# A recurrent attention and a silu layer on one core: the first eight units in another order on all engines, u loaded as one row

## The chip, the cores and the metric

The kernel runs on one core of a Trainium2 chip. The metric is the device time of one execution in microseconds (us), as the median of several runs. Engines are named as in the profile: PE (TensorE; PEld is its weight load), DVE (VectorE), ACT (ScalarE), POOL (GpSimd) and SP (SyncE, which here only issues DMAs).

## The reference

A linear attention with a decayed state is followed by a two-layer network. All inputs and the output are float32; batch 4, 8 heads, 768 steps, head size 48, hidden size 2048.

```python
def _attn_ref(r, k, v, w, u):
    state = zeros((B, H, D, D)); y = zeros_like(r)
    for t in range(S):
        kt, vt, rt = k[:, :, t], v[:, :, t], r[:, :, t]
        cur = einsum('bhd,bhe->bhde', u[None] * kt, vt)
        y[:, :, t] = einsum('bhd,bhde->bhe', rt, state + cur)
        state = w[None, :, :, None] * state + einsum('bhd,bhe->bhde', kt, vt)
    return y

def _moe_ref(x, w_in, w_out):          # x: y as (3072, 384)
    h = x @ w_in
    return (h * (1.0 / (1.0 + exp(-h)))) @ w_out
```

## The kernel before, in words

The sequence is cut into 6 chunks of 128 steps. A unit is one chunk of one batch entry with all 8 heads; unit i is chunk i // 4 of batch entry i % 4, so there are 24 units, and the first eight are the first two chunks. Each unit loads three tiles of 192 KB (`rin`, `kin`, `vin`, in 8 buffers each).

For a unit, PE turns r and k (line 258, 16 transposes: T), DVE multiplies them by powers of w (line 270: rT, kT), PE multiplies r by k (line 321 for the first four units, P or A; line 394 for the others in pairs, D), DVE masks the product (n, m), and PE multiplies it by v (V, or Z with the state). The term with u goes another way: POOL multiplies k by r (line 226, ku) and by u (line 231, ru), DVE sums over the head (line 239, rd), POOL multiplies v by that sum (line 244, vu), and DVE adds it when it takes y from PSUM (line 342: e, z). POOL also decays k for the state (line 234, kc); PE sums k times v into states (S for the first chunk, Q later). ACT casts v (v16), evicts the transposed y (xT) and applies silu. y is turned on PE (line 525, yT) for the first six units, and by DMA later.

The network's first layer on a chunk (line 540: L and H) needs y of that chunk turned and a quarter of w_in (i_q0 to i_q3; the steps with the numbers 12 to 15 use the last quarter); its silu is G. The second layer (line 562) needs w_out (i_o0 to i_o3). POOL issues the weights, each as a DMA that casts to float16. SP issues the loads of r, k and v.

The instructions of each engine run in the order in which the program states them; there is no scheduler. For the first eight units that order is one written list of words (`order`, near line 650): a word names a step and a unit, and each step's instructions go to the end of their engines' queues. Behind the list a loop takes the units from the seventh on in pairs, and fills TensorE's time with pieces of the two layers left over (`fillers`). `n*spin` puts n matmuls on idle data on PE; `clear` is four such matmuls. A load is `lr`, `lk` or `lv` on SP's queue; `ak` is k on ACT's queue. At most eight of these DMAs are in flight: each takes one of eight semaphores in turn, and its queue waits until the DMA that had it before has landed. PSUM tiles tagged "moe" share four buffers in the order of the list.

`pd`, `pa` and `kz` clear the pads of the 48-wide heads (rin and kin on DVE or ACT, kc on POOL); `cz` clears tiles for pairs of states; `mh` makes maskH from maskM on POOL by two copies. The powers of w come from `wpT` (two small loads), over `lnw` (ACT: logarithm and lamR), `eK` (DVE) and `lamK` (ACT); `wr` loads w as one row, which `wb` spreads over 128 partitions by a matmul with ones.

Of the kernel before, what the change touches and what calls it, by code (L numbers as in the profile page):

```python
# [15 lines left out]
def kernel(  # L16
# [175 lines left out]

    def spread_u():
        nc.scalar.dma_start(out=u_bc, in_=bass.AP(tensor=u.tensor, offset=0,
                                                  ap=[[0, 128], [D, H], [1, D]]))

    def copy_u(copy=nc.vector.tensor_copy):
# [35 lines left out]
    def decayed_k(i, eng=nc.gpsimd):  # L233
        eng.tensor_tensor(out=kc[i % NIN][:, :, 0:D], in0=kin[i % NIN][:, :, 0:D],  # L234
                          in1=lamH if unit(i)[0] else lamC, op=ALU.mult)

# [14 lines left out]
    def turn_one(i, x):  # L251
# [3 lines left out]
        for p in range(NP):  # L255
            for y in range(2):
                rows = slice(HC * y, HC * y + HC)
                nc.tensor.transpose(L(i)["t"][0:PR, y, x, p, :], flat[rows, 128 * p:128 * p + PR],  # L258
                                    ident[rows, rows])

    def decay_one(i, x, key=None):
# [6 lines left out]
        lam = (lam[:, :, 0:HC].unsqueeze(1).broadcast_to([PR, 2, NP, HC]) if unit(i)[0]  # L268
               else lam.rearrange("p g (y t) -> p y g t", y=2))
        nc.vector.tensor_tensor(  # L270
            out=L(i)[key].rearrange("p g (y t) -> p y g t", y=2),
            in0=L(i)["t"][0:PR, :, x], in1=lam, op=ALU.mult)

    def early(i):
        return unit(i)[0] == 1

# [25 lines left out]

    def cast_r(i, copy=nc.vector.tensor_copy):
        L(i)["rT16"] = wrk.tile([PR, NP, C], F16, name="rT16", bufs=4)
        copy(out=L(i)["rT16"], in_=L(i)["rT"])

# [69 lines left out]
    def spread_first(i, copy=nc.vector.tensor_copy):  # L376
        spread_pairs(copy, carry_pairs[i // 2], L(i)["sps"])

# [46 lines left out]
    def w_half():  # L425
        return wHT.unsqueeze(1).unsqueeze(3).broadcast_to([PR, 2, NP, D])

    def state_first(i):
        s1 = L(i)["s1"] = wrk.tile([PR, 2, NP, D], FP, name="s1")
        nc.vector.tensor_tensor(out=flat(s1), in0=L(i)["sp"][0][0:PR, 0:HD],  # L430
                                in1=flat(L(i)["sdec"]), op=ALU.add)
        if early(i):
            spread_pairs(nc.scalar.copy, inner_pairs[i // 2 % 2], s1)
            return
        for j in range(2):
            spread_state(nc.scalar.copy, j, inner[i // 2 % 2], s1)

    def state_second(i):
        sc, b = unit(i)
        if sc == NCH - 1:  # L440
            return
        s2 = L(i)["sp"][1][0:PR, 0:HD].rearrange("p (e g n) -> p e g n", e=2, g=NP)
        for p in range(NP):
            nc.vector.scalar_tensor_tensor(
                out=st[b // 2][:, :, p, :], in0=L(i)["s1"][:, :, p, :], scalar=wHT[:, p:p + 1],
                in1=s2[:, :, p, :], op0=ALU.mult, op1=ALU.add)

# [17 lines left out]
    def outputs_halves(i):  # L465
# [8 lines left out]
        if early(i):  # L474
            for p in range(NP):
                for e in range(2):
                    for x in (e, 1 - e):
                        s = inner_pairs[i // 2 % 2] if x else carry_pairs[i // 2 - 2]
# [11 lines left out]
        for p in range(NP):  # L490
            for j in range(2):
                h = 2 * p + j
                for e in range(2):
                    for x in range(2):
                        r = HC * x
                        nc.tensor.matmul(place(e, x, D * h, D), L(i)["am2"][r:r + HC, j, e, p, :],  # L496
                                         L(i + e)["v16"][r:r + HC, h, :],
                                         start=False, stop=True, skip_group_check=True)

# [122 lines left out]
    def piece(word, f):  # L622
# [5 lines left out]
        "id16": lambda: nc.gpsimd.tensor_copy(out=ident16, in_=ident), "itr": row_numbers,  # L628
        "itc": column_numbers, "mk": mask, "mh": half_mask, "wr": lambda: row(w_row, w),
        "lnw": powers_r, "eK": exponents_k, "lamK": powers_k,  # L630
        "wb": lambda: spread_row("w", w_row), "lnwb": ln_w, "lamC": powers_c, "lamH": powers_h,
        "tab": silu_table, "ud": spread_u, "clear": clear, "spin": lambda: None,
        "H": lambda: halved.pop(0)(),
    }
    unit_steps = {
        "T": turn, "rT": lambda i: decay_one(i, 0), "kT": lambda i: decay_one(i, 1),
        "v16": cast_v, "kc": decayed_k, "vu": bonus_v, "ku": bonus_ku, "ru": bonus_rku,
        "rd": bonus_sum, "D": product_halves, "A": lambda i: product(i, i + 1), "n": masked,
        "m": masked_halves, "V": outputs_y, "e": evict_first, "S": first_sums, "st": first_state,
        "sc": spread_first, "yT": turn_y, "xT": copy_x,  # L640
        "xTD": lambda i: copy_x(i, nc.vector.tensor_copy),
        "rA": lambda i: cast_r(i, nc.scalar.copy), "sd": decayed_state, "i_q": ld_win,
        "i_o": ld_wout, "Q": sums, "s1_": state_first, "s2_": state_second, "sn": next_state,
        "sx": next_crossed, "Z": outputs_halves, "z": evict_halves, "lr": lambda i: ld(i, rin, r),
        "lk": lambda i: ld(i, kin, k), "lv": lambda i: ld(i, vin, v),
        "ak": lambda i: ld(i, kin, k, nc.scalar), "pd": pad, "pa": pad_copy,
        "kz": lambda i: nc.gpsimd.memset(kc[i][:, :, D:64], 0.0), "cz": zero_state,
    }
    order = """
        id itr itc lr0 mk id16 wr ak0 ud lr1 lk1 lv0 kz2 lr2 lv1 pd1 pd2 lv2 lk2 cz2 pd0 lr3  # L650
        lk3 kz3 cz1 kz0 kz1 pd3 cz3 kz5 kz6 kz7 cz0 mh lnw eK kz4 lv3 lamK clear lr4 lk4 lv5
        lv4 lr5 lk5 lr6 lk6 lk7 lr7 6*spin lv7 lv6 T0 ku0 rT0 kT0 3*spin T1 rT1 kT1 v160 ru0
        rd0 ku1 pa5 wb v161 A0 ru1 rd1 n0 vu0 lnwb lamC vu1 lamH tab pa4 pa6 pa7 n1 2*spin
        V0 e0 i_q0 T2 kT2 4*spin V1 ku2 yT0 ru2 rT2 xTD0 T3 rT3 e1 i_q1 1*spin yT1 xT1 v162
        kT3 ku3 ru3 rd2 A2 vu2 i_q2 3*spin v163 rd3 vu3 n2 n3 L0.0 G0.0 V2 L0.2 G0.2 e2 V3
        e3 L0.4 yT2 G0.4 kc1 xT2 yT3 kc0 xT3 L0.6 G0.6 S0 sc0 st0 kc2 L2.2 L2.0 L2.4 T4 L2.6
        rT4 kT4 kc3 G2.0 G2.2 ku4 G2.4 v164 G2.6 L4.8 S2 sc2 st2 i_q3 ru4 rA4 G4.8 L4.10
        L4.9 rd4 kc5 sd4 G4.10 L4.11 T5 G4.9 kc4 G4.11 vu4 ku5 kT5 ru5 i_o0 rT5 v165 Q4 D4
        s1_4 m4 rd5 s2_4 rA5 L4.12 G4.12 vu5 i_o1 L4.13 G4.13 Z4 z4 L4.14 G4.14 L4.15 G4.15
        yT4 xT4 i_o2 yT5 xT5 T6 kT6 v166 rT6 kc6 ku6 rA6 H H ku7 H kc7 T7 rT7 v167 rA7 H kT7  # L660
        H ru7 ru6 rd6 sd6 i_o3 vu6 sn4 sx4
    """
    for word in order.split():
# [85 lines left out]
```

## Time and profile before

| | |
|---|---|
| median of 3 runs | 189.76 us (189.26 to 190.07) |
| the profiled execution's own time | 190.19 us |
| its span in the trace | 188.5 us |
| TensorE busy | 178.8 us (95%) |
| VectorE, ScalarE, GpSimd busy | 115.8, 108.0, 111.3 us |
| read from HBM, written | 20.65 MB, 4.72 MB |

Times in a timeline or a chain count from the start of the span. In a timeline row stand the start, the length, the engine (an engine's name with q is its instruction queue, where DMAs are issued), the line, the operation, what it writes and reads, how many, and in brackets how long the engine stood before it and what it waited for. In a group row stand the total, the mean of one in ns, and the idle time before them.

### The profile page before, as it was taken

The page shows a single profiled execution, that of the slowest core. Times are in us where ns is not written, and L with a number is a line of the kernel's source. Part 1 is how long each engine was busy: PE and PEld are TensorE (multiplying, and loading weights), DVE is VectorE, ACT ScalarE, POOL GpSimd, SP SyncE. Part 2 cuts the span into 40 slices and gives each one's busy share as a digit, 9 for nine tenths or more (in the row PEclk, how much of TensorE's full clock was granted, in tenths as well). Part 3 has the DMA queues.
Part 4 walks back from the last instruction along what each step waited for, and adds up shares of the span by engine and source line. Part 5 has one row for each costly group of instructions (what it writes and reads, how often), then busy time and mean ns, then how long its engine had stood idle before and what let it go on. Part 6 is the DMA issues. An engine that isn't in the chain of part 4 may idle for free.

```text
span 188.5 us, 6820 instructions
## 1 busy us (share of the span) xinstructions
PE 178.8 (95%) x2915; PEld 117.3 (62%) x2915; DVE 115.8 (61%) x221; ACT 108.0 (57%) x214; POOL 111.3 (59%) x145
## 2 busy tenths in 40 slices
PE   7788999999899999999999999999999999999992
PEld 2355885679666896656656655656746666555662
DVE  7389847857796693697675696755883955000120
ACT  5157569569433397158695268695268592289200
POOL 8599997799899837738639547659349130000000
PEclk9999999999999999999999999999999999999998
DMA  5899999999959368369177287185386201410012
GB/s 88 170 200 181 230 182 185 180 211 193 187 101 207 139 129 164 109 132 208 46 145 172 68 164 193 37 175 129 89 168 171 45 3 45 125 42 0 17 70 85
DMA packets 88737, 24.44 MB, mean 130 GB/s; under 512 B 83329, under 2 KB 88194, under 8 KB 88706
## 3 DMA queue, kind: packets, MB, share of 16 engines
q1 hardware_dynamic: 84992, 20.39, 49.5%
q0 software_dynamic: 2176, 3.15, 10.3%
q10 hardware_dynamic: 1538, 0.46, 1.1%
q8 instruction: 23, 0.38, 0.8%
q14 instruction: 8, 0.07, 0.1%
HBM read 20.65 MB, written 4.72 MB: 135 GB/s over the span
## 4 chain that ended last, share of the span: by engine, by line
PE 84%; DMA 8%; DVE 3%; ACT 2%; issue 1%; SPq 1%; DVEq 0%
PE ops L562 32%; PE hps L540 32%; DMA kin<-in_k_dram 8%; PE att L258 6%; PE att L394 4%; PE att L321 2%; PE yp L487 2%; PE sp L417 2%; PE ops L587 1%; PE yp L496 1%; PE zs L167 1%; DVE kT L270 1%; DVE am L327 1%; PE yp L337 1%; ACT gT L549 1%
## 5 line engine op out<-in xcount | busy, mean ns | idle before, releaser
L540 PE MATMUL hps<-xT,win 128*128 128x512 f16 (+1 forms) x360 | 66.6, 337 | 0.1
L549 ACT ACTIVATE gT<-hps 128x512 f16<-128x512 f32 x96 | 56.0, 597 | 14.7 <-PE hps L540 11.3
L562 PE MATMUL ops<-wout,gT 128*128 128x384 f16 x368 | 62.5, 326 | 0.0
L540 PEld LDWEIGHTS <-win 128*128 128x128 f16 x360 | 38.9, 114 | 21.3 <-issue 0.3
L562 PEld LDWEIGHTS <-gT 128*128 128x128 f16 x368 | 35.2, 98 | 23.3
L244 POOL TENSOR_TENSOR vu<-vin,rku 128x384 f32<-128x384 f32 x24 | 19.6, 830 | 28.0 <-DVE rku L239 27.5
L270 DVE TENSOR_TENSOR rT<-att,lamR 112x512 f32<-112x512 f32 (+1 forms) x40 | 27.1, 685 | 6.7 <-PE att L258 6.2
L226 POOL TENSOR_TENSOR ku<-kin,rin 128x384 f32<-128x384 f32 x24 | 24.1, 1006 | 9.6 <-DMA kin<-in_k_dram 9.5
L568 ACT COPY osb<-ops 128x384 f32<-128x384 f32 x20 | 9.6, 479 | 34.5 <-issue 18.1
L342 DVE TENSOR_TENSOR y<-yp,vu 64x384 f16<-64x384 f32 (+1 forms) x34 | 18.9, 555 | 14.9 <-PE yp L496 6.8
L231 POOL TENSOR_TENSOR rku_f<-ku,u_bc 128x384 f32<-128x384 f32 x24 | 24.0, 1001 | 2.1 <-DMA u_bc<-in_u_dram 0.5
L234 POOL TENSOR_TENSOR kc<-kin,lamH 128x384 f16<-128x384 f32 x20 | 20.1, 1005 | 0.7 <-DMA kin<-in_k_dram 0.6
L270 DVE TENSOR_TENSOR kT<-att,lamK 112x512 f32<-112x512 f32 x24 | 16.3, 681 | 1.5 <-PE att L258 1.5
L249 ACT CAST v<-vin 128x384 f16<-128x384 f32 x24 | 11.5, 512 | 6.6 <-DMA vin<-in_v_dram 6.4
L430 DVE TENSOR_TENSOR s<-sp,sdec 112x384 f32<-112x384 f32 x10 | 5.6, 557 | 15.9 <-PE sp L417 15.7
L570 DVE COPY osb<-ops 128x384 f32<-128x384 f32 x3 | 1.7, 558 | 21.3 <-PE ops L562 21.3
L401 DVE TENSOR_TENSOR am<-att,maskH 128x1024 f16<-128x1024 f32 x10 | 12.2, 1218 | 1.5 <-PE att L394 1.5
L239 DVE TENSOR_REDUCE rku<-rku_f 128x8 f32<-128x384 f32 x24 | 12.4, 544 | 0.6 <-POOL rku_f L231 0.6
L394 PE MATMUL att<-rT,kT 48*64 48x64 f32 x640 | 11.8, 220 | 0.3 <-DVE rT L270 0.3
L258 PE MATMUL att<-ident,rin 64*112 64x64 f32 x192 | 10.3, 228 | 1.0 <-DMA rin<-in_r_dram 1.0
L373 ACT CAST s1h<-s 48x384 f16<-48x384 f32 x16 | 8.2, 510 | 5.4 <-DVE s L430 5.2
L394 PEld LDWEIGHTS att<-rT,kT 48*64 48x64 f32 x640 | 10.5, 135 | 0.5 <-DVE rT L270 0.5
(83 smaller groups left out, 173.8 us busy)
## 6 DMA issues: line engine op xcount, KB each, us to landing
rin<-in_r_dram SPq DMA_DIRECT2D x24, 192.0 KB, 4.3
vin<-in_v_dram SPq DMA_DIRECT2D x24, 192.0 KB, 4.1
kin<-in_k_dram SPq DMA_DIRECT2D x23, 192.0 KB, 4.3
out_dram<-osb SPq DMA_DIRECT2D x23, 192.0 KB, 3.0
win<-in_moe_w_in_dram POOLq DMA_DIRECT2D x4, 384.0 KB, 6.2
wout<-in_moe_w_out_dram POOLq DMA_DIRECT2D x4, 384.0 KB, 6.3
xT<-y SPq DMA_TRANSPOSE x18, 2.4
kin<-in_k_dram ACTq DMA_DIRECT2D x1, 192.0 KB, 4.1
```

What stands on the lines that cost most here:

```text
L226: eng.tensor_tensor(out=L(i)["ku"], in0=kin[i % NIN][:, :, 0:D], in1=rin[i % NIN][:, :, 0:D], op=ALU.mult)
L231: eng.tensor_tensor(out=L(i)["rku_f"], in0=L(i)["ku"], in1=u_bc, op=ALU.mult)
L234: eng.tensor_tensor(out=kc[i % NIN][:, :, 0:D], in0=kin[i % NIN][:, :, 0:D], in1=lamH if unit(i)[0] else lamC, op=ALU.mult)
L239: nc.vector.tensor_reduce(out=L(i)["rku"], in_=L(i)["rku_f"], axis=mybir.AxisListType.X, op=ALU.add)
L244: eng.tensor_tensor(out=L(i)["vu"], in0=vin[i % NIN], in1=L(i)["rku"].unsqueeze(2).broadcast_to([128, H, D]), op=ALU.mult)
L258: nc.tensor.transpose(L(i)["t"][0:PR, y, x, p, :], flat[rows, 128 * p:128 * p + PR], ident[rows, rows])
L270: nc.vector.tensor_tensor(out=L(i)[key].rearrange("p g (y t) -> p y g t", y=2), in0=L(i)["t"][0:PR, :, x], in1=lam, op=ALU.mult)
L342: nc.vector.tensor_tensor(out=y16[a], in0=y[b, 0:HD], in1=vu[a], op=ALU.add)
L394: nc.tensor.matmul(a[o0:o0 + HC, j, e, p, :], kT[r0:r0 + D, p, HC * x:HC * x + HC], rT[r0:r0 + D, p, HC * x:HC * x + HC], start=True, stop ...
L540: nc.tensor.matmul(hps[:, f, :], win[(ft + f) // 4].rearrange("p q (t c) -> p q t c", c=4) [:, q, :, (ft + f) % 4], xts[sc][:, q, b0:b0 + ...
L549: nc.scalar.activation(out=gts[sc][:, ft:ft + m, b0 * C:(b0 + nb) * C], in_=hpss[b0, ft], func=AF.Silu)
L562: nc.tensor.matmul(opss[b], gts[sc][:, ft, b * C:(b + 1) * C], wout[:, ft, :], start=(ft == 0), stop=(ft == NFT - 1))
```

## The change

The order of the first eight units is written anew; every engine does the same steps on them with these differences.

- u is loaded as one row of 1.5 KB on ACT's queue (`ur`), spread by a matmul with ones (`ub`) and copied from PSUM by DVE (`uc`). Before, ACT's queue loaded it into all 128 partitions (`ud`).
- r of units 1 and 2 is loaded on ACT's queue (`ar`), r of unit 0 ahead of the small load of w on SP's queue, and k of unit 4 ahead of k of units 1 and 2.
- The first y transposes stand back to back (`yT0 yT1`), with y of unit 1 taken from PSUM before rT of unit 3 is made.
- Idle matmuls (`spin`) go from 19 to 5. The products of units 0 and 1, and 2 and 3, come one after the other and not interleaved.
- The pads and clears are spread differently over DVE, ACT and POOL (`pg` and `cg` are on POOL), `mh` stands behind `ku0`, and kc of units 1 and 5 come earlier on POOL.
- Copies change engine: xT of unit 0 from DVE to ACT, xT of units 2 and 3 from ACT to DVE; r of unit 7 is cast on DVE, and r of unit 6 is made a second time from PSUM on DVE (`rP`), each in place of a cast on ACT.
- The loads of units 8 and 9 stand in the list, k of unit 9 ahead of v of unit 8; before, they followed it.

Other edits (`in_halves`, `summed`, the condition in `early`) give the same instructions for these units as before.

```diff
-    columns(nc.sync, wpT, w, 1)
-    columns(nc.scalar, wpT, w, 0)
...
-    def spread_u():
-        nc.scalar.dma_start(out=u_bc, in_=bass.AP(tensor=u.tensor, offset=0,
-                                                  ap=[[0, 128], [D, H], [1, D]]))
...
+        "itc": column_numbers, "mk": mask, "mh": half_mask, "ur": lambda: row(u_row, u),
+        "wr": lambda: row(w_row, w), "wx": lambda: columns(nc.sync, wpT, w, 1),
+        "wy": lambda: columns(nc.scalar, wpT, w, 0), "lnw": powers_r, "eK": exponents_k,
+        "lamK": powers_k, "uc": copy_u, "wb": lambda: spread_row("w", w_row),
+        "ub": lambda: spread_row("u", u_row), "lnwb": ln_w, "lamC": powers_c, "lamH": powers_h,
...
-        id itr itc lr0 mk id16 wr ak0 ud lr1 lk1 lv0 kz2 lr2 lv1 pd1 pd2 lv2 lk2 cz2 pd0 lr3
-        lk3 kz3 cz1 kz0 kz1 pd3 cz3 kz5 kz6 kz7 cz0 mh lnw eK kz4 lv3 lamK clear lr4 lk4 lv5
-        lv4 lr5 lk5 lr6 lk6 lk7 lr7 6*spin lv7 lv6 T0 ku0 rT0 kT0 3*spin T1 rT1 kT1 v160 ru0
-        rd0 ku1 pa5 wb v161 A0 ru1 rd1 n0 vu0 lnwb lamC vu1 lamH tab pa4 pa6 pa7 n1 2*spin
-        V0 e0 i_q0 T2 kT2 4*spin V1 ku2 yT0 ru2 rT2 xTD0 T3 rT3 e1 i_q1 1*spin yT1 xT1 v162
-        kT3 ku3 ru3 rd2 A2 vu2 i_q2 3*spin v163 rd3 vu3 n2 n3 L0.0 G0.0 V2 L0.2 G0.2 e2 V3
-        e3 L0.4 yT2 G0.4 kc1 xT2 yT3 kc0 xT3 L0.6 G0.6 S0 sc0 st0 kc2 L2.2 L2.0 L2.4 T4 L2.6
-        rT4 kT4 kc3 G2.0 G2.2 ku4 G2.4 v164 G2.6 L4.8 S2 sc2 st2 i_q3 ru4 rA4 G4.8 L4.10
-        L4.9 rd4 kc5 sd4 G4.10 L4.11 T5 G4.9 kc4 G4.11 vu4 ku5 kT5 ru5 i_o0 rT5 v165 Q4 D4
-        s1_4 m4 rd5 s2_4 rA5 L4.12 G4.12 vu5 i_o1 L4.13 G4.13 Z4 z4 L4.14 G4.14 L4.15 G4.15
-        yT4 xT4 i_o2 yT5 xT5 T6 kT6 v166 rT6 kc6 ku6 rA6 H H ku7 H kc7 T7 rT7 v167 rA7 H kT7
-        H ru7 ru6 rd6 sd6 i_o3 vu6 sn4 sx4
+        kz3 wy id itr mk wr ur pd1 id16 itc pd3 lr0 pg0 cz3 ak0 wx lk4 ar1 lk1 cg0 lk2 kz5
+        lv0 cz1 lnw lv1 lv2 kz0 lr3 lk3 lr4 eK kz6 lamK lv3 kz2 pg7 clear lk5 lv4 lr5 cg2
+        kz4 ar2 kz7 lv5 ub uc 1*spin T0 pg2 lk6 wb ku0 mh T1 ru0 rT0 v160 kT0 ku1 ru1 P0 kT1
+        lr7 rd0 kz1 rT1 P1 n0 rd1 V0 vu0 lnwb v161 pd5 lr6 lamC i_q0 lamH lv7 lk7 n1 T2 kT2
+        e0 lv6 vu1 ku2 1*spin V1 T3 rT2 e1 i_q1 3*spin rT3 kT3 ru2 pa4 ku3 rd2 yT0 yT1 ru3
+        xT1 xT0 P2 v162 P3 tab i_q2 L0.2 n2 pa6 rd3 n3 G0.2 v163 kc1 vu2 vu3 V2 L0.0 G0.0
+        kc2 kc0 V3 kc5 ku4 kc3 i_q3 e2 e3 L0.6 L0.4 yT3 G0.6 yT2 G0.4 xTD3 T4 xTD2 S0 st0
+        sc0 L2.2 rT4 v164 kT4 L2.4 G2.4 G2.2 L2.6 ru4 kc4 ku5 T5 S2 st2 rT5 v165 L4.8 rd4
+        sd4 ru5 G2.6 sc2 G4.8 L2.0 G2.0 L4.10 G4.10 L4.11 G4.11 L4.9 Q4 G4.9 vu4 kT5 D4 rA4
+        s1_4 rd5 rA5 L4.12 i_o0 G4.12 m4 s2_4 vu5 Z4 ku6 i_o2 z4 i_o1 L4.13 G4.13 L4.14 yT4
+        xT4 L4.15 v167 yT5 lr8 lk8 xT5 kc6 G4.15 lr9 T7 i_o3 T6 rT6 rP6 v166 kT6 rT7 kT7
+        G4.14 ru6 H lk9 ku7 lv9 kc7 sd6 H r167 rd6 H H ru7 lv8 sx4 sn4 H vu6
...
-    load(8)
-    load(9)
```

More of the change, by code (lines that the diff above doesn't have):

```diff
@@ L476, in outputs_halves @@
                 for e in range(2):
-                    for x in (e, 1 - e):
+                    for x in (e, 1 - e) if unit(i)[0] else (1,):
                         s = inner_pairs[i // 2 % 2] if x else carry_pairs[i // 2 - 2]
@@ L644 @@
[L644 to L647, printed above, removed]
+        "rd": bonus_sum, "D": product_halves, "P": product, "n": masked, "m": masked_halves,
+        "V": outputs_y, "e": evict_first, "S": first_sums, "st": first_state, "sc": spread_first,
```

48 lines of the change are left out of this document (27 added, 21 removed).

## The prediction

> **What bounds the kernel now.** I read the page first, then the busy time by stages, then the chain of waits, then the timeline of the first 60 us. The page:
>
> ```profile
> PE 178.8 (95%) x2915; PEld 117.3 (62%) x2915; DVE 115.8 (61%) x221; ACT 108.0 (57%) x214; POOL 111.3 (59%) x145
> DMA  5899999999959368369177287185386201410012
> ```
>
> TensorE is busy for 95% of the span, so time can only come from the other 5% or from work that TensorE need not do. The DMA engines are full in the first eleven slices of 4.7 us, some 52 us, and not after. The busy times of three stages (columns: stretch, its length, then PE, PEld, DVE, ACT and POOL):
>
> ```profile
> 31.00:41.00 10.00, 8.94 (x206) 6.02 (x205) 7.72 (x17) 6.83 (x14) 8.29 (x11) 1.00 1.07 198
> 41.00:52.00 11.00, 10.13 (x243) 8.64 (x242) 7.97 (x16) 7.48 (x15) 10.18 (x13) 1.00 1.02 191
> 52.00:60.00 8.00, 8.00 (x106) 4.91 (x107) 5.88 (x12) 2.36 (x5) 7.84 (x10) 1.00 0.71 138
> ```
>
> From 52 us on TensorE has no gap (8.00 of 8.00), while in the 21 us before it misses 1.06 + 0.87 us. What the change does to the time is therefore how much earlier TensorE enters the stretch that begins at about 51.5 us, and that is decided by what arrives last in the opening. Four pieces of the chain that ended last:
>
> ```profile
> 2.52 6.63 DMA kin<-in_k_dram
> ...
> 27.46 0.59 PE att L258 x16
> ...
> 43.36 7.62 DMA kin<-in_k_dram
> ...
> 51.47 7.91 PE ops L562 x48
> ```
>
> It begins with a load (k of unit 1) and passes through a second one (k of unit 9) just before the full stretch.
>
> **The opening: loads, u, the first y.**
>
> ```profile
> 2.01 0.41 ACTq L72 DMA_DIRECT2D kin<-in_k_dram  x1
> ...
> 2.44 0.60 ACTq L194 DMA_DIRECT2D u_bc<-in_u_dram  x1
> ...
> 5.49 2.86 SPq L72 DMA_DIRECT2D rin<-in_r_dram  x1
> ...
> 6.21 1.00 POOL L226 TENSOR_TENSOR ku<-kin,rin 128x384 f32<-128x384 f32 x1 [1.00 <-DMA kin<-in_k_dram]
> ...
> 7.73 1.00 POOL L231 TENSOR_TENSOR rku_f<-ku,u_bc 128x384 f32<-128x384 f32 x1 [0.52 <-DMA u_bc<-in_u_dram]
> ...
> 17.64 0.55 DVE L342 TENSOR_TENSOR y<-yp,vu 128x384 f16<-128x384 f32 x1
> ...
> 21.18 0.82 PE L540 MATMUL hps<-xT,win 128*128 128x256 f16 x6
> ```
>
> u: the broadcast load and its 0.60 us on ScalarE's queue go; a load of one row, one matmul and one copy on VectorE come instead. The group rows that price these and all that follows (busy us, mean ns of one):
>
> ```profile
> L226 POOL TENSOR_TENSOR ku<-kin,rin 128x384 f32<-128x384 f32 x24 | 24.1, 1006 | 9.6 <-DMA kin<-in_k_dram 9.5
> L231 POOL TENSOR_TENSOR rku_f<-ku,u_bc 128x384 f32<-128x384 f32 x24 | 24.0, 1001 | 2.1 <-DMA u_bc<-in_u_dram 0.5
> L234 POOL TENSOR_TENSOR kc<-kin,lamH 128x384 f16<-128x384 f32 x20 | 20.1, 1005 | 0.7 <-DMA kin<-in_k_dram 0.6
> L244 POOL TENSOR_TENSOR vu<-vin,rku 128x384 f32<-128x384 f32 x24 | 19.6, 830 | 28.0 <-DVE rku L239 27.5 <-DMA vin<-in_v_dram 0.2
> ...
> L270 DVE TENSOR_TENSOR rT<-att,lamR 112x512 f32<-112x512 f32 x24 | 16.5, 686 | 6.5 <-PE att L258 6.2
> ...
> L239 DVE TENSOR_REDUCE rku<-rku_f 128x8 f32<-128x384 f32 x24 | 12.4, 544 | 0.6 <-POOL rku_f L231 0.6
> ...
> L342 DVE TENSOR_TENSOR y<-yp,vu 128x384 f16<-128x384 f32 x14 | 7.8, 555 | 14.5 <-PE yp L496 6.8 <-POOL kc L234 4.6 <-POOL rku_f L231 3.1
> ...
> L327 DVE TENSOR_TENSOR am<-att,maskM 128x1024 f16<-128x1024 f32 x4 | 4.7, 1220 | 1.3 <-PE att L321 1.3
> ...
> L83 POOL DMA_DIRECT2D win<-in_moe_w_in_dram x4 | 3.3, 836 | 0.0
> ...
> L141 POOL COPY maskH<-maskM 64x64 f32<-64x64 f32 x2 | 1.0, 499 | 0.1
> ...
> L191 PE MATMUL bc<-w_row,ones 1*128 1x384 f32 x2 | 0.9, 533 | 0.0
> ...
> L144 DVE MEMSET s1p<- 112x384 uint32 x2 | 0.8, 378 | 0.1
> ```
>
> The matmul costs 0.53 us, and the copy about 0.56 (the row of a VectorE operation that reads 384 columns of PSUM). Both lie ahead of the first transposes, where TensorE and VectorE wait for kin anyway; I count them as nothing, and 0.5 us if the row of u lands only after kin does. The first product with u loses its wait of 0.52.
>
> r of units 1 and 2 move to ScalarE's queue. Ahead of the exponentials stands a load that may hold ScalarE between 0.41 us (row at 2.01) and 2.86 us (row at 5.49, an issue that the queue held up). I take 0.6, the row at 2.44, which is on the same queue at the same time. The exponentials then end near 6 us and the first rT starts near 7 with kin, as the page has it now; at 2.86 rT would start 1 us later, of which 0.5 reaches the end, since GpSimd's chain (next) has the other half covered. SP loses two issues ahead of the k and v loads, and k of unit 4 is put before k of unit 1. One load of 192 KB fewer stands in the stream.
>
> VectorE's order puts the sum of y of unit 1 ahead of rT of unit 3 (now behind it). The first ku comes at 6.5, not 6.21, since k of unit 0 is issued behind one more small load. GpSimd's added clearings (three pairs of pads, two pair tiles) lie ahead of it, where it now idles 1.00 us and where the maskH copies, 1.0 us, go away; at 0.38 for a pair tile and less for a pad they need about 2 us and just fit. From the first rku_f, which then ends at 9.5 (ku, two maskH copies at 0.50, rku_f), VectorE does rku, rT, am, rku, two fills, am, kT, y, rT, y: 0.54 + 0.69 + 1.22 + 0.54 + 0.3 + 1.22 + 0.69 + 0.56 + 0.69 + 0.56 = 7.0, which ends at 16.5. Now this y ends at 17.64 + 0.55 = 18.2. So the two transposes of y, back to back, come 1.7 us earlier, and with them the first matmuls of the first layer (21.18 now, near 19 then; the first quarter of w_in, issued by GpSimd near 12.4 instead of 13.3, lands in time). The fourteen idle matmuls that go fill gaps of TensorE and cost nothing.
>
> **The second stage: GpSimd sets the pace.** That gain isn't kept. GpSimd's order to the last vu of the first four units holds 4 ku, 4 rku_f, 4 vu, 3 issues of w_in, the two maskH copies and one kc: 4.02 + 4.00 + 3.32 + 2.51 + 1.00 + 1.01 = 15.9, from 6.5 to 22.4. Two more kc bring it to 24.4, when the first state sums (S0) can start. Now:
>
> ```profile
> 15.68 3.21 SPq L72 DMA_DIRECT2D kin<-in_k_dram  x1
> ...
> 24.88 0.43 PE L358 MATMUL sp<-v,kc 128*64 128x48 f16 x16
> ...
> 26.49 0.80 POOL L83 DMA_DIRECT2D win<-in_moe_w_in_dram  x1
> ...
> 28.98 1.00 POOL L234 TENSOR_TENSOR kc<-kin,lamH 128x384 f16<-128x384 f32 x1 [0.65 <-DMA kin<-in_k_dram]
> ...
> 34.86 1.48 PE L540 MATMUL hps<-xT,win 128*128 128x512 f16 x6
> ...
> 36.77 0.82 POOL L244 TENSOR_TENSOR vu<-vin,rku 128x384 f32<-128x384 f32 x1 [1.21 <-DVE rku L239]
> ```
>
> S0 gains 24.88 - 24.4 = 0.5 us, and the 16 transposes of unit 4 (0.59 in the chain), which now follow S0, are done before it: TensorE leads by 1.1. Then GpSimd has kc of unit 5, ku of unit 4 and kc of unit 3, 3.0 us, before it issues the last quarter of w_in at 27.4 (now 26.49). Landing times of w_in and kin, from the views of these tiles:
>
> ```profile
> DMA to landing us min/median/max: 5.7/6.2/7.0
> ```
> ```profile
> DMA to landing us min/median/max: 3.2/4.3/10.3
> ```
>
> So the last quarter lands at 27.4 + 6.2 = 33.6 (33.1 to 34.4), and the first matmul on it (step L4.12, now at 34.86) gains 1.3 us, between 0.5 and 1.8. TensorE is there in time: from S0 to L4.12 it now takes 9.98, less 0.59 for the moved transposes 9.4, so that it would come at 33.8 with every gap that it has now and earlier without them. Behind L4.12 both orders hold the same matmuls up to 44 us; GpSimd's wait of 1.21 before vu of unit 5 goes, since VectorE's rku of that unit now stands ahead of the mask, and vu then ends near 35 instead of 37.6. So the lead of 1.3 is kept up to the chain's second load: k of unit 9 is now issued at 43.36, as the 30th big load counting u, and holds TensorE until 51.0. In the new order it is the 28th, two loads sooner; at 1.0 us each (192 KB at the 198 GB/s of the stage from 31 us) that is 2.0, enough for the lead.
>
> Sum: -1.3 us. The profiled execution took 190.19 (span 188.5 and 1.7 around it), so 188.9 on that scale; it lies 0.43 above the median of 189.76, so the median goes to 188.5.
>
> **The rivals.**
>
> Slower: k of unit 5 is late. The new order puts kc of unit 5 on GpSimd at 24.4, ahead of kc of unit 3 and of the issue of the last quarter of w_in. In the row at 28.98 that same operation waits for its load even now. If the load comes at 28.98 again, the issue moves to 28.98 + 3.0 = 32.0, w_in lands at 38.2, and L4.12 is 3.3 later than now: 193.1. It decides from 24.4 + 1.3 = 25.7 on. Against it: k of unit 5 is the 15th big load in the new order, the 19th now; the present 15th is the load issued at 15.68, and with kin's landings (4.3 median, 10.3 at most, 7.6 for the load in the chain) it is there at 20.0 to 26.0, 23.3 by the chain's row. Chance 0.2.
>
> No change: k of unit 9 lands at 51.0 as now, because the weights, issued earlier, take the DMA engines from it. TensorE then waits at the same place for the whole lead: 189.8. For it: the DMA row is full up to there. Chance 0.17.
>
> No change by the clock. These rows are idle matmuls of one size, before and after TensorE came to full pace, and the products of units 2 and 3:
>
> ```profile
> 2.97 2.77 PE L167 MATMUL zs<-idle 128*128 128x512 f16 x6
> ...
> 6.58 0.82 PE L167 MATMUL zs<-idle 128*128 128x512 f16 x3
> ...
> 18.51 2.07 PE L321 MATMUL att<-rT,kT 48*64 48x128 f32 x64
> ```
>
> They go at 0.46 and then 0.27 us apiece. Now TensorE works without a gap from 1.3 to 6; in the new order it stands from about 3 to 6.5 but for two matmuls, and may stay at the slow pace. If it does until the products, these take 2.1 us more and the first layer begins at 21 as now; of the lead about 0.6 is left after the wait for w_in: 189.2. Chance 0.11. The Trainium skill, page "TensorE: Matmul & The Clock Gate", Part 1, has this as a rule: half pace until a window of some 3.4 us has been busy, and again after an idle one. By that rule fewer idle matmuls speak against this change; the trace agrees that the pace rises after some 5 us of work, and its gaps of up to 1.5 us afterwards don't bring the slow pace back, so that no row here shows a fall.
>
> **How the numbers follow.** About 0.5%, 0.95 us, is what can be told from no change here. The forecast, 0.52, is 188.5 with its own range of 188.0 to 189.3 (1.8 and 0.5 us of lead). It is faster but for its upper end; I put 0.02 of it in the middle. Faster 0.50; within, 0.02 + 0.17 + 0.11 = 0.30; slower 0.20. The range must reach into the slower case: its price runs from 189.8 at the deciding point to 193.1, and I go halfway, 191.4. Below I add the 0.87 us that TensorE misses from 41 to 52 to the forecast, against the chance that it goes in part: 187.4.
>
> **What would show it.** Right: the two transposes of y near 16.6 and S0 near 24.4; GpSimd without a wait for kin before kc of unit 5; the last issue of w_in near 27.4 and the first matmul on it near 33.6; the stretch without gaps from about 50. Wrong: GpSimd waiting for kin at 24 to 29, a wait of the transposes for kin that ends at 51 again, or idle matmuls and products at the slow pace after 10 us. A stall of ScalarE over 1 us at the load of r would show the bound of the second part.

## The result and the profile after

The changed kernel takes 187.41 us (median of 11 runs, 186.94 to 188.91). The kernel before, run beside it, takes 189.26 (11 runs, 187.66 to 192.42). The ratio is 0.9916, with a 95% interval of 0.9889 to 0.9943: 0.8% faster. Every ratio here is formed from executions in the fast state alone, so it is not the quotient of the two medians. The profiled execution of the changed kernel took 187.48, with a span of 185.8 (before: 190.19 and 188.5). The two profiles lie 2.7 us apart and the medians only 1.85, since before's profiled execution is 0.93 above the median of the runs beside it and the changed kernel's 0.07.

The page of the changed kernel, the two lines that answer to those of before:

```profile
PE 178.6 (96%) x2903; PEld 118.8 (64%) x2903; DVE 117.2 (63%) x221; ACT 106.0 (57%) x207; POOL 112.7 (61%) x153
DMA  5999999999189287278285287293395201410022
```

TensorE is busy as long (178.6 us for 178.8: fourteen idle matmuls fewer, but slower products, as the rows below show) in a span that is 2.7 us shorter: the time came out of its gaps. The busy times by stage say where (columns as before):

```profile
31.00:41.00 10.00, 8.77 (x212) 6.28 (x211) 7.06 (x15) 7.96 (x16) 9.95 (x13) 1.00 1.08 193
41.00:52.00 11.00, 10.97 (x235) 8.88 (x234) 10.30 (x20) 6.49 (x14) 9.16 (x12) 1.00 0.63 124
52.00:60.00 8.00, 8.00 (x138) 5.16 (x137) 6.84 (x15) 2.74 (x6) 7.84 (x10) 1.00 0.96 220
```

From 41 us on TensorE has almost no gap (10.97 of 11.00; before 10.13), and the DMA engines, full until 52 us before, have room (share 0.63 for 1.02). The chain that ended last, the pieces that matter:

```profile
2.30 4.68 DMA kin<-in_k_dram
...
27.89 6.60 DMA win<-in_moe_w_in_dram
...
49.24 7.91 PE ops L565 x48
...
180.27 2.65 PE ops L590 x32
```

The second load of before's chain, k of unit 9, is gone from it. The last quarter of w_in stands there instead. The second layer's long stretch begins at 49.24 (51.47 before), 2.23 us earlier, and the last group starts at 180.27; before, that group stood at

```profile
182.53 2.65 PE ops L587 x32
```

2.26 us later. So 2.23 of the 2.7 us between the two spans have been made by about 50 us; the last 0.4 lies behind the last copy of the output, which stands 2.26 us apart too (185.20 and 182.94). The rows of the opening in the changed kernel, in the order of the steps of the prediction:

```profile
7.12 1.00 POOL L220 TENSOR_TENSOR ku<-kin,rin 128x384 f32<-128x384 f32 x1 [0.95 <-DMA kin<-in_k_dram]
8.07 0.52 POOL L139 COPY maskH<-maskM 64x64 f32<-64x64 f32 x2
8.67 1.00 POOL L225 TENSOR_TENSOR rku_f<-ku,u_bc 128x384 f32<-128x384 f32 x1
...
10.32 3.88 PE L319 MATMUL att<-rT,kT 48*64 48x128 f32 x64
10.44 0.69 DVE L267 TENSOR_TENSOR kT<-att,lamK 112x512 f32<-112x512 f32 x1 [1.25 <-PE att L252]
...
15.72 0.69 DVE L267 TENSOR_TENSOR kT<-att,lamK 112x512 f32<-112x512 f32 x1 [0.20 <-PE att L252]
...
17.39 0.55 DVE L340 TENSOR_TENSOR y<-yp,vu 128x384 f16<-128x384 f32 x1
...
17.61 0.72 PE L528 MATMUL yT<-ident,y 128*128 128x128 f16 x6
18.27 2.01 PE L319 MATMUL att<-rT,kT 48*64 48x128 f32 x64
20.21 0.85 PE L543 MATMUL hps<-xT,win 128*128 128x256 f16 x6
...
25.00 1.00 POOL L228 TENSOR_TENSOR kc<-kin,lamH 128x384 f16<-128x384 f32 x1
25.10 0.43 PE L356 MATMUL sp<-v,kc 128*64 128x48 f16 x16
27.89 0.80 POOL L83 DMA_DIRECT2D win<-in_moe_w_in_dram  x1
...
32.15 1.15 PE L392 MATMUL att<-rT,kT 48*64 48x64 f32 x64
33.07 1.81 SPq L72 DMA_DIRECT2D kin<-in_k_dram  x1
34.53 0.84 PE L543 MATMUL hps<-xT,win 128*128 128x512 f16 x3 [1.23 <-DMA win<-in_moe_w_in_dram]
34.76 0.84 POOL L238 TENSOR_TENSOR vu<-vin,rku 128x384 f32<-128x384 f32 x1
```

The stations of the opening are 0.2 to 1.4 us later than I had put them. The first matmul on the last quarter of w_in (step L4.12) comes at 34.53: a lead of 0.33, not 1.3. TensorE itself was ready for it at 33.30 (the end of the row at 32.15), 1.56 ahead of before; 1.23 of that it waited for w_in. In this profile the lead comes back behind L4.12. From L4.12 to the state sums of unit 4 (step Q) before took 9.49 us, the changed kernel 8.47; from there to the 48 matmuls of the second layer it is 7.05 and 6.17. The rows of before, then of the changed kernel:

```profile
38.67 0.33 PE L525 MATMUL yT<-ident,y 128*128 128x128 f16 x3
39.26 0.34 PE L525 MATMUL yT<-ident,y 128*128 128x128 f16 x3 [0.26 <-DVE y L342]
...
44.35 0.44 PE L417 MATMUL sp<-v,kc 64*64 64x48 f16 x32
...
51.03 0.44 PE L258 MATMUL att<-ident,kin 64*112 64x64 f32 x8 [0.87 <-DMA kin<-in_k_dram]
51.40 0.82 PE L562 MATMUL ops<-wout,gT 128*128 128x384 f16 x4
```
```profile
43.00 0.44 PE L415 MATMUL sp<-v,kc 64*64 64x48 f16 x32
...
48.86 0.39 PE L252 MATMUL att<-ident,kin 64*112 64x64 f32 x8
49.17 3.10 PE L565 MATMUL ops<-wout,gT 128*128 128x384 f16 x18
```

0.87 of the second difference is the wait for k of unit 9, which is gone. The sum is 0.33 + 1.02 + 0.88 = 2.23. This is the split in one execution; in a second profile of the same kernel (the third set below) it is 1.33 + 1.02 + 0.40 = 2.75. Nor is the 1.02 the gain of the new order alone: in a run with the same words behind L4.12 and no wait for w_in (the first y turned apart), that stretch takes 9.20.

### The profile page after: what moved, and what is told of

Its sections match the earlier page's. It is cut to its first block, busy times and chain, and to the rows that moved or that the text cites. A ratio compares the mean times of both kernels' runs of the same rounds, so it can differ in the third digit from the quotient of the medians.

```text
span 185.8 us, 6793 instructions
## 1 busy us (share of the span) xinstructions
PE 178.6 (96%) x2903; PEld 118.8 (64%) x2903; DVE 117.2 (63%) x221; ACT 106.0 (57%) x207; POOL 112.7 (61%) x153
## 4 chain that ended last, share of the span: by engine, by line
PE 80%; POOL 10%; DMA 6%; issue 2%; ACT 0%; ACTq 0%; POOLq 0%
PE ops L565 33%; PE hps L543 30%; PE att L252 5%; PE att L392 5%; DMA win<-in_moe_w_in_dram 4%; POOL ku L220 3%; DMA kin<-in_k_dram 3%; POOL rku_f L225 2%; POOL kc L228 2%; PE sp L415 2%; POOL vu L238 2%; PE yp L489 2%; PE yp L498 2%; PE ops L590 1%; POOL win L83 1%
## 5 line engine op out<-in xcount | busy, mean ns | idle before, releaser
L252 PE MATMUL att<-ident,rin 64*112 64x64 f32 x192 | 10.8, 236 | 0.0
L252 PE MATMUL att<-ident,kin 64*112 64x64 f32 x192 | 10.1, 228 | 0.5 <-DMA kin<-in_k_dram 0.5
```

## The experiments

Three sets of four kernels ran, each set on one chip with the kernel before. The theory formed from these traces: the opening brings little by itself, and the time comes from the new order behind L4.12 and from the earlier load of k of unit 9. Its rival is the prediction's sum: the opening's lead is what is left at the end. The changed kernel itself ran beside before and in the third set, not in the first two, so there a run is held against it by the ratios to before.

**The loads alone.** The kernel before, with only the loads of units 8 and 9 in the new sequence.

```diff
-    load(8)
-    load(9)
+    for word in ("r8 k8 r9 k9 v9 v8").split():
+        ld(int(word[1]), {"r": rin, "k": kin, "v": vin}[word[0]], {"r": r, "k": k, "v": v}[word[0]])
```

> The old order with one thing of the new: k of unit 9 is loaded before v of units 8 and 9. Theory A (a good part of the gain is the wait for k of unit 9, 0.87 us at 51 us, and it goes when this load is asked for earlier): the wait before the transposes of unit 9 gets shorter, by up to 0.87 us, and the time falls by 0.4 to 0.9. Rival B (that load is late because the weights of the second layer hold the DMA engines from 36 to 49 us, so that one place in the queue does little): the load lands at 50 or later, the time changes by less than 0.4.

Measured: 188.63 against 189.80 (ratio 0.9953, 0.9918 to 0.9988). In its trace L4.12 stands at 35.03, no earlier than before, and the second layer's stretch begins earlier by 0.9:

```profile
50.48 2.77 PE L562 MATMUL ops<-wout,gT 128*128 128x384 f16 x16
```

By the ratios about half of the gain, in the traces 0.9 of 2.23 us, needs nothing of the opening. k of unit 9 is issued at 36.80 here, at 43.36 before: v of unit 8 no longer stands ahead of it on SP's queue. That load waits for its buffer, by the queue's waits from 25 to 50 us in the kernel before:

```profile
SPq L72 <- ACT v L249: 3.2, 1, 3.2
```

**u broadcast again.** The changed kernel with u loaded into all partitions, its issue behind k of unit 0.

```diff
-"ur": lambda: row(u_row, u),
+"ur": spread_u,
...
-        kz3 wy id itr mk wr ur pd1 id16 itc pd3 lr0 pg0 cz3 ak0 wx lk4 ar1 lk1 cg0 lk2 kz5
+        kz3 wy id itr mk wr pd1 id16 itc pd3 lr0 pg0 cz3 ak0 ur wx lk4 ar1 lk1 cg0 lk2 kz5
...
-        kz4 ar2 kz7 lv5 ub uc 1*spin T0 pg2
+        kz4 ar2 kz7 lv5 1*spin T0 pg2
```

> The new order, but u is again loaded into all 128 partitions by ScalarE's queue, behind k of unit 0; the row, its matmul and the copy are gone. If u as a row carries the gain: 1 us or more slower than the new kernel. If it was only moved off the path: the loads behind it come 0.5 to 1 us later, the first rku_f on GpSimd waits for u as in the old kernel, and as GpSimd's chain leads to the last quarter of w_in, the time rises by 0.3 to 1.0.

Measured: 188.81 (ratio to before 0.9977, 0.9941 to 1.0012), so by the ratios more than half of the gain is lost. TensorE's waits up to 53 us:

```profile
PE att L256 <- DMA kin<-in_k_dram: 2.0, 1, 2.0
PE att L256 <- DMA rin<-in_r_dram: 1.5, 2, 1.3
```

The changed kernel waits 0.5 there for kin and not at all for rin. The wait for kin is no loss: the transposes behind it start at 6.47 here and at 7.12 in the changed kernel, where the matmul on the row of u fills the time before. The wait for rin is one: the transposes of unit 1 start at 10.05 (9.29), and GpSimd's second ku waits 0.96 for the same load. The first product with u does not wait. So the row of u does more than take away the first wait for u: r of unit 1 lands sooner, which fits the 192 KB fewer ahead of it on its queue. The stretch of the second layer begins at 49.98, 0.8 later than with the row.

**r of units 1 and 2 on SP's queue**, at the same places of the list.

```diff
-... ak0 wx lk4 ar1 lk1 cg0 lk2 kz5
+... ak0 wx lk4 lr1 lk1 cg0 lk2 kz5
...
-        kz4 ar2 kz7 lv5 ub uc 1*spin T0
+        kz4 lr2 kz7 lv5 ub uc 1*spin T0
```

> The new order, but r of units 1 and 2 is loaded by SP's queue, at the same places in the list. If ScalarE's queue brings these loads sooner: the transposes of unit 1 start later than 9.3 us, the time rises by 0.3 or more. If all the loads share the DMA engines anyway: r of unit 1 lands within 0.5 us of now, and the time is the same within 0.3 us.

Measured: 196.02 (ratio 1.0339, 1.0292 to 1.0387). None of the expectations held (the transposes of unit 1 start at 8.71, sooner than in the changed kernel), and the reason is in two rows:

```profile
14.04 4.95 SPq L72 DMA_DIRECT2D rin<-in_r_dram  x2
...
22.23 0.68 PE L252 MATMUL att<-ident,rin 64*112 64x64 f32 x8 [8.17 <-DMA rin<-in_r_dram]
```

r of unit 2 is behind fifteen loads of 192 KB on SP's queue (the next expectation says twelve), and it is the second of the two in the row at 14.04: it is issued at 18.14. On ScalarE's queue, which holds few, it was issued at 7.38. A place in the list is not a place in time when the queue changes. So the run says what the second queue is worth at this place, not what it is worth at all. Hence the next one.

**r on SP's queue, r of unit 2 ahead of the loads of v.**

```diff
-... ak0 wx lk4 ar1 lk1 cg0 lk2 kz5
+... ak0 wx lk4 lr1 lk1 cg0 lk2 lr2 kz5
...
-        kz4 ar2 kz7 lv5 ub uc 1*spin T0
+        kz4 kz7 lv5 ub uc 1*spin T0
```

> The new order with r of units 1 and 2 on SP's queue as before, but r of unit 2 placed ahead of the v loads of units 0 to 2 and not behind twelve loads. If it was the late place in SP's queue that cost 7.6 us and not the queue: the transposes of unit 2 start within 1 us of 14.6 and the time comes back to within 0.5 of the new kernel. If ScalarE's queue itself is worth something: it stays 1 us or more slower.

Measured: 187.42 (ratio to before, which was 188.82 in this set, 0.9948, 0.9916 to 0.9979); the second layer's stretch begins at 49.13. The transposes of unit 2 start at 14.36. By the medians this kernel and the changed one are alike (187.41); by the ratios they are 0.3% apart, with intervals that overlap. So the queue as such is worth little, if anything; what counts is that r of unit 2 comes ahead of the loads of v.

**The first y turned apart.** The changed kernel with y of unit 0 turned before the transposes of unit 3, and y of unit 1 after them.

```diff
-        e0 lv6 vu1 ku2 1*spin V1 T3 rT2 e1 i_q1 3*spin rT3 kT3 ru2 pa4 ku3 rd2 yT0 yT1 ru3
-        xT1 xT0 P2
+        e0 lv6 vu1 ku2 1*spin V1 yT0 T3 rT2 xT0 rT3 e1 i_q1 3*spin kT3 ru2 pa4 ku3 rd2 yT1 ru3
+        xT1 P2
```

> The new order, but the first two y are turned apart as in the old one: y of unit 1 is taken behind rT of unit 3, and its transposes come later. If the place of y decides: the first matmuls of the first layer move from 20.2 to 21 us and the time rises by 0.5 to 1. If GpSimd's chain sets the pace behind it: the state sums stay at 25.1 and the last quarter of w_in lands when it does now, and the time is the same within 0.3 us.

Measured: 188.17 (ratio to before 0.9932, 0.9897 to 0.9967). The first matmul of the first layer comes at 21.88 (20.21), S0 at 26.59 (25.10), L4.12 at 34.72 (34.53), the second layer's stretch at 49.88 (49.17). Of 1.5 us lost in the opening 0.2 is left at L4.12, where the changed kernel waits for w_in, and 0.7 at 50 us; the ratios differ by 0.0016, or 0.3 us, within their intervals. So neither expectation holds in full: S0 moves, and the time hardly does. L4.12 does not wait here, and then TensorE waits at Z instead, for ScalarE's cast of r:

```profile
36.27 0.23 PE L481 MATMUL yp<-s1p,rT 112*64 112x96 f16 x1 [0.44 <-ACT rT L303]
```

From L4.12 to Q it takes 9.20, with the words of the changed kernel (8.47) and against 9.49 before. So of the 1.02 some 0.3 is what the new order saves when nothing is late, and 0.7 is a wait at Z that the wait for w_in covers.

**More idle matmuls ahead of u.** The changed kernel with four more.

```diff
-        kz4 ar2 kz7 lv5 ub uc 1*spin T0
+        kz4 ar2 kz7 lv5 4*spin ub uc 1*spin T0
```

> The new order with four more idle matmuls between the four first ones and the matmul of u, so that TensorE works without a gap from 1.3 to about 7.8 us. Clock theory (the fewer idle matmuls keep TensorE at half pace to 16 us and that costs time): full pace comes near 6.3, the products of units 0 and 1 take 2.0 us and not 3.9, the state sums start 0.5 us or more before 25.1, and the time falls by 0.5 to 1. Cover theory (at half pace this work still fits beside GpSimd's chain): the products get fast but GpSimd's last issue of w_in moves by less than 0.3 us, and the time stays within 0.3.

Measured: 187.04 (ratio to before 0.9930, 0.9901 to 0.9959). In the profiled execution the clock did not rise any earlier (the 64 products of units 0 and 1 took 3.88 us there too), so its trace says nothing on what half pace costs. Its twelve runs do, in part. Seven took 186.64 to 187.05, and the mean granted clock recorded for them is 0.972 or 0.982; five took 187.72 to 188.39 with 1.000, the profiled one (187.91) among them. A mean below 1 says here that the clock fell at some time after it had risen, as in a trace shown below. Four idle matmuls seem to have been enough in some runs only, and the two kinds lie 1 us apart. That the clock makes this difference is likely and not shown, since the faster kind has no trace.

**The last quarter of w_in earlier.** The changed kernel with its issue two GpSimd operations earlier, and the next step on it ahead of Z.

```diff
-        kc2 kc0 V3 kc5 ku4 kc3 i_q3 e2 e3
+        kc2 kc0 V3 kc3 i_q3 kc5 ku4 e2 e3
...
-        ... vu5 Z4 ku6 i_o2 z4 i_o1 L4.13 G4.13 L4.14 yT4
+        ... vu5 L4.13 G4.13 Z4 ku6 i_o2 z4 i_o1 L4.14 yT4
```

> The new order with the issue of the last quarter of w_in two GpSimd operations earlier (kc of unit 3 and the issue ahead of kc of unit 5 and ku of unit 4), and the matmuls L4.13 ahead of Z4. If the last quarter of w_in is what the new order waits for: it is issued near 26.0 and lands near 32.5, the wait of 1.23 us before L4.12 goes, and the time falls by 0.6 to 1.2. If something behind it is as late (the masked product of units 4 and 5, the casts of their r): the wait moves to Z4 or to the layer behind, and the time falls by less than 0.4. If the earlier transfer delays k and v of the next units, it is slower.

Measured: 187.95 (ratio to before 0.9945, 0.9911 to 0.9980). L4.12 comes at 33.23, without the wait for w_in, 1.3 earlier than in the changed kernel. But the waits of TensorE up to 53 us now include

```profile
PE yp L481 <- ACT gT L552: 0.4, 1, 0.4
PE yT L528 <- DVE y L340: 0.2, 1, 0.2
```

and the second layer's stretch begins at 48.86, 0.3 earlier. The time did not fall (the changed kernel's ratio is 0.9916). What stands behind w_in is only little less late: with the products ahead of L4.12 at the same place (32.15 in both), L4.12 1.3 earlier is worth 0.3. Part of this may be the edit's second half: with L4.13 ahead of Z the stretch from L4.12 to Q takes 9.49, as before. This run doesn't tell the two apart.

**The old order behind L4.12.** The changed kernel with before's words from there on, and the loads in the new sequence.

```diff
-        ... L4.12 i_o0 G4.12 m4 s2_4 vu5 Z4 ku6 i_o2 z4 i_o1 L4.13 G4.13 L4.14 yT4
...
+        ... L4.12 G4.12 vu5 i_o1 L4.13 G4.13 Z4 z4 L4.14 G4.14 L4.15 G4.15
+        yT4 xT4 i_o2 yT5 xT5 T6 kT6 ... H H ku7 H kc7 T7 rT7 ...
```

> The new order up to the sums of units 4 and 5, and from there the old one (mask ahead of rku of unit 5, Z4 behind L4.13, transposes of unit 7 among the first layer's matmuls), with the loads of units 8 and 9 at the end of the list in the new sequence. If the new order of this stretch carries some 0.9 of the lead: from L4.12 to the first matmuls on y of unit 4 it takes 0.5 to 0.9 longer, and the time rises by that. If it only follows from earlier inputs: the same within 0.3 us.

Measured: 187.85 (ratio to before 0.9959, 0.9935 to 0.9983). L4.12 stands at 33.80 here, behind a wait of 0.86 for w_in, and the state sums of unit 4 at 43.12: 9.32 us, close to before's 9.49, where the changed kernel behind a like wait takes 8.47. So with w_in late the new order saves 0.85 between these two stations. At the end less is seen of it. The second layer's stretch begins at 49.08 and the last group at 180.08, no later than in the changed kernel's first profile (49.17 and 180.27), since L4.12 came 0.73 earlier in this execution. The time is 0.43 above the kernel with r on SP's queue, which ran beside it and has the changed kernel's order here: a ratio of 1.0023, 0.9985 to 1.0043 by resampling the runs. That lies between the two expectations, and that this order is worth time is not shown. In the rows, the 1.02 between before and the changed kernel is made of pieces: the wait for y and the restart behind it (yT4 to T6: 0.86 before, 0.47 after), Z (1.07 and 0.83), and the transposes of units 6 and 7 in one row instead of two (1.33 and 1.04).

**The third set: the changed kernel again, and three edits of it.**

> The changed kernel itself again, beside the three below, so that each can be held against it on the same chip. Expected as in its first runs: about 187.4 us, the first product of the second layer in its 48-column form near 49.2 us from the span's start, 2.2 us ahead of the kernel before, and TensorE at half pace until about 16 us.

Measured: 187.38 (6 runs, 187.11 to 187.66); before was 189.58 in this set (ratio 0.9876, 0.9832 to 0.9920). Its profile shows how far a station can be trusted:

```profile
6.60 1.00 POOL L220 TENSOR_TENSOR ku<-kin,rin 128x384 f32<-128x384 f32 x1 [0.42 <-DMA kin<-in_k_dram]
...
33.53 0.84 PE L543 MATMUL hps<-xT,win 128*128 128x512 f16 x3 [0.74 <-DMA win<-in_moe_w_in_dram]
...
45.75 0.82 PE L565 MATMUL ops<-wout,gT 128*128 128x384 f16 x4 [0.24 <-DVE st L446]
...
48.65 1.64 PE L565 MATMUL ops<-wout,gT 128*128 128x384 f16 x9
```

The same program had k of unit 0 half a microsecond earlier in this execution, and L4.12 1.0 earlier. Of this 1.0, all is left at Q (42.00), 0.5 at the second layer's stretch, 0.28 at the last group (179.99), and the execution took 187.33 instead of 187.48. The lead of the opening runs out on the way, here behind Q.

**A dense start.** Eight idle matmuls right behind the four that clear the banks, then u.

```diff
-        kz4 ar2 kz7 lv5 ub uc 1*spin T0
+        kz4 ar2 kz7 lv5 8*spin ub uc T0
```

> The changed kernel with eight idle 512-column matmuls right behind the four that clear the banks, with no row of u between them, and none between u's row and unit 0's transposes. Theory 'the clock needs an unbroken stretch of wide matmuls, and half pace costs the opening': TensorE reaches full pace near 6.3 us, as in the kernel before; the 64 products of units 0 and 1 take about 2.0 us instead of 3.9, y of unit 1 comes up to 0.8 us earlier, and the time is near 186.8 us (0.3 to 0.8 below the changed kernel). Theory 'GpSimd's chain sets the opening': pace comes back, the products take 2.0 us, and the first w_in matmul, the first state products and the time stay within 0.3 us of the changed kernel. If the products still take 3.9 us, this run says nothing on the cost of the pace, but that twelve wide matmuls in a row are not enough for it.

Measured: 186.95 (ratio to the changed kernel beside it 0.9977, 0.9957 to 1.0003 by resampling the runs). The busy times of its first 20 us (PEclk is the third number from the end):

```profile
2.00:6.00 4.00, 4.00 (x11) 1.32 (x9) 1.40 (x3) 1.78 (x7) 3.82 (x19) 1.00 1.06 199
6.00:10.00 4.00, 3.97 (x58) 2.32 (x58) 2.52 (x5) 0.79 (x3) 3.37 (x7) 0.94 1.22 241
10.00:16.00 6.00, 5.97 (x95) 4.71 (x91) 5.66 (x11) 2.44 (x8) 5.88 (x9) 0.50 1.12 199
16.00:20.00 4.00, 4.00 (x89) 3.24 (x86) 3.83 (x7) 2.40 (x4) 3.90 (x5) 0.95 1.25 222
```

(The 1.00 of the first row holds for lack of a record: idle matmuls went at 0.43 us there.) The clock rose at 6.1 us, fell again at 9.5 and came back at 16.4, while TensorE had work all the time. So the products were slow again (3.79 us), and the run tests the price of half pace up to 9.5 us only: 0.4 us, with an interval that still includes no change. The trace shows how it comes about. VectorE has kT of unit 1 without a wait, sums the first rku at 9.94 (10.52 in the changed kernel beside it) and ends y of unit 1 0.59 earlier. That lead is 0.78 at L4.12 (32.75), 0.56 at the second layer's stretch (48.09) and 0.21 at the last group (179.78).

**k of unit 0 first.** On ScalarE's queue ahead of everything.

```diff
-        kz3 wy id itr mk wr ur pd1 id16 itc pd3 lr0 pg0 cz3 ak0 wx
+        kz3 ak0 wy id itr mk wr ur pd1 id16 itc pd3 lr0 pg0 cz3 wx
```

> The changed kernel with k of unit 0 as the first transfer of ScalarE's queue, ahead of w's column and the rows of w and u. Theory 'the opening lead was lost on k of unit 0, which landed 0.6 us later than I had put it': the first ku starts at about 6.2 us instead of 7.1, u's products follow 0.5 to 0.9 us earlier, the last quarter of w_in is issued 0.5 us earlier, and the time is near 186.9 us. Rival 'r of unit 1, which lands at 9.0 us, sets the second ku, and what follows hangs on that': the first ku is earlier, the second starts at 9.0 to 9.6 us, and the time is within 0.3 us of the changed kernel. A loss of some 0.5 us would mean that the decay powers, whose column of w now comes later, hold up unit 0.

Measured: 188.53 (ratio to the changed kernel beside it 1.0062, 1.0047 to 1.0081): slower. The first ku is as early as hoped, and then GpSimd waits:

```profile
6.14 1.00 POOL L220 TENSOR_TENSOR ku<-kin,rin 128x384 f32<-128x384 f32 x1
...
8.65 1.00 POOL L220 TENSOR_TENSOR ku<-kin,rin 128x384 f32<-128x384 f32 x1
...
12.17 0.83 POOL L238 TENSOR_TENSOR vu<-vin,rku 128x384 f32<-128x384 f32 x1 [1.30 <-DVE rku L233]
```

VectorE stands before rku with rT and kT of unit 0, which came later since the rows of w and u, and so TensorE's queue (u's spread at 5.11 us, 3.98 in the changed kernel beside it), came later. The theory that k of unit 0 alone cost the lead falls: the small loads are as urgent. And this loss is not made up on the way: L4.12 comes 1.17 later (34.70), the second layer's stretch 1.04 (49.69), the last group 1.26 (181.25).

**All three edits of the changed kernel that could gain**: the dense start, k of unit 0 first, and w_in earlier.

> The two edits above, and the last quarter of w_in two GpSimd operations earlier with the matmuls on it two pieces earlier, together. If each takes away a wait of its own (opening pace, k of unit 0, the transfer of w_in), their gains add: 186.0 to 186.5 us, the first 48-column product of the second layer near 48.2 us. If one wait stands behind all three (the states of units 4 and 5, made on VectorE and ScalarE), it is no faster than the best of them alone: 186.8 to 187.2 us, that product near 48.9 us.

Measured: 186.60 (6 runs, 186.28 to 187.26; ratio to the changed kernel beside it 0.9958, 0.9942 to 0.9982; to before 0.9838, 0.9796 to 0.9879). It beats both kernels. In this profile the clock stayed up, and the products took 2 x 1.09 us:

```profile
9.68 1.09 PE L319 MATMUL att<-rT,kT 48*64 48x128 f32 x32
11.49 1.09 PE L319 MATMUL att<-rT,kT 48*64 48x128 f32 x32 [0.73 <-DVE rT L267]
...
32.47 1.49 PE L543 MATMUL hps<-xT,win 128*128 128x512 f16 x6
...
48.37 1.80 PE L565 MATMUL ops<-wout,gT 128*128 128x384 f16 x10
```

L4.12 is 1.1 us earlier than in the changed kernel of this set, the second layer's stretch 0.3, and the last group 0.62 (179.37). The time lies between the two expectations, a little nearer to that of gains that add (186.0 to 186.5). But they are not gains of each edit: alone, the dense start gave 0.4 us, k of unit 0 first cost 1.2, and w_in earlier gave nothing that its run can tell. What the three have together is a start at full pace, and how much of the 0.8 us is the clock's is not told apart here.

## Why the prediction was right, and where it was not

The forecast of 188.5 pointed the right way, and its range of 187.4 to 191.4 only just holds the 187.41 measured; that it does is luck. I had a gain of 1.3 us; it was 1.85 between the medians and 2.7 between the profiled executions. The step that failed is "the lead of 1.3 is kept up to the chain's second load", with the pricing of what follows it at nothing.

- **The opening's chain.** First ku at 6.5: 7.12, and 6.60 in the second profile. First rku_f ending at 9.5: 9.67 and 9.13. Sum of y of unit 1 ending at 16.5: 17.94 and 17.4. S0 at 24.4: 25.10 and 24.59. Last quarter of w_in issued at 27.4: 27.89 and 27.38, on the engine at 33.6: 34.53 and 33.53. That GpSimd sets the pace was right: the chain that ended last is GpSimd's from the first ku at 7.12 to the issue at 27.89, and from that ku to S0 it took 17.98 us (forecast 17.9). VectorE's list was right too, 6.90 us from the first rku to y of unit 1 (7.0), but not its start: the first rku begins at 11.04, not at 9.5, since VectorE makes kT of unit 1 ahead of it and waits 1.25 for the transposes (row at 10.44). The lead at L4.12, predicted 1.3, is 0.33 in one execution and 1.33 in the other. Half of the difference is when k of unit 0 lands, the other half the transfer of w_in (6.60 and 6.11 us). One profile can't tell such a step to better than 0.5 to 1 us.
- **"Kept up to the chain's second load."** I named GpSimd's wait of 1.21 before vu of unit 5, and that VectorE sums rku ahead of the mask, yet gave it no time since both orders hold the same matmuls. The stretch became 1.02 shorter. With the old order there it takes 9.32 for 8.47, and with the new one and no wait for w_in 9.20: some 0.3 is the order alone, the rest a wait at Z that goes when w_in is late. What failed is the belief that what follows L4.12 is the same for both.
- **k of unit 9: "two loads sooner ... enough for the lead".** I counted places in the stream, 2.0 us. It is issued 10.3 us sooner (33.07, was 43.36), 6.6 of them by the sequence of the last six loads alone, as the run with the loads alone shows (36.80), since SP's queue no longer stands ahead of it at a load of v that waits for its buffer. The whole wait of 0.87 went. I had this amount only at the end of the range, as "the chance that it goes in part"; it was a term of the sum.
- **What the opening's lead is worth.** I took each microsecond at L4.12 as one at the end. For what comes earlier the runs show less: 1.0 became 0.5 at 50 us, 0.28 at the last group and 0.15 in the execution's time (the two profiles of the changed kernel), and 0.78 became 0.56 and 0.21 (the dense start). For what comes later it holds: 1.17 became 1.04 and 1.26 (k of unit 0 first). So the opening is not free, as the theory of the first traces had it; something else is nearly as late. This error worked against the other two, and the total came out nearer than its terms.
- **The rival of k of unit 5** did not occur: GpSimd's row at 25.00 stands without a wait. **k of unit 9 as late as before** did not either. **The clock** did what that rival says: the products of units 0 and 1 took 3.88 us and those of units 2 and 3, at 18.27, 2.01. Its price was set too high in the end: I had 0.7 us against the forecast, on the belief that the first layer then starts at 21, and it started at 20.21. VectorE's own list of operations was last at y of unit 1, and in its last 4 us before that sum it waited for TensorE once, 0.20 us (row at 15.72). What half pace costs shows earlier, in the wait of 1.25 for kT of unit 1, which the dense start does not have. The gaps of up to 1.5 us that I gave for the kernel before are those of the weight loads; its matmuls stand 1.05 us at most after the rise. The run that mends part of it gives 0.4 us, and 1 us lies between the two kinds of runs with four more idle matmuls. The Trainium skill, page "TensorE: Matmul & The Clock Gate", Part 1, says that the gate judges a free-running window of some 3.4 us. The trace of the dense start agrees: full pace from 6.1 to 9.5 us, which is one such window.
- **Costs put at nothing.** The copy of u and the row's matmul are hidden, as said, though the matmul took 1.61 us at half pace and not 0.53, which is the mean of its two records. The maskH copies took 0.52 us for both and not 1.0. ScalarE's stall at the load of r stayed under 1 us (issue of 0.40 us for r of unit 1).

## What to carry to other kernels

Count a moved load by what stands before it on its own queue and what those instructions wait for, not by its place in a list or the bytes ahead of it: here one move by itself was worth 6.6 us of issue time and another cost over 8 us of run time. A lead won early in a kernel is a gain only if the next thing to arrive comes earlier as well, while a loss can be felt in full, so price every wait between the edit and the point where the bottleneck has no more gaps, and add those that go. Where an opening hangs on loads, compare two profiles of the same kernel before a step of half a microsecond is believed.

## What the runs showed of the hardware that was not expected

TensorE fell back to half pace while it was never idle. In the dense start it worked for 5.97 of the 6.00 us from 10 to 16 us at a granted clock of 0.50, on small fp32 transposes and on products of 48 rows; before those it had run for 3.4 us at full pace. The run with the loads alone shows the like: a granted clock of 0.72 from 10 to 16 us, with TensorE busy for 5.78 of 6.00. The Trainium skill, page "TensorE: Matmul & The Clock Gate", Part 4, says that transposes don't count as busy for the gate in the way that matmuls do. The trace of the dense start fits as far as the fall goes: between 7.2 and 9.5 us TensorE did 32 transposes and one matmul on a single row. But the 64 products kept the slow pace for another window, and what in them does not count stays open. The kernel with all three edits issues the same work 0.4 us later and kept full pace in its profile; so a kernel with little dense work at its start can fall on either side by where the window stands, and that may be why runs of some kernels lie in two groups 1 us apart.
